# Sparse attention and a gated feed-forward layer on one core: the first 21 transfers wait for the landing of the third one ahead

## The chip, the cores and the metric

One core of a Trainium2 chip. The time is the device time of one execution in microseconds (us), the median of several runs. TensorE is called PE, VectorE DVE, ScalarE ACT, GpSimd POOL, and SyncE, which issues nearly all transfers of this kernel, SP.

## The reference, cut to what matters

```python
# q, k, v: 8 batches, 8 heads, 576 positions, head size 64, f32
scores = q @ k.T / sqrt(64)
# heads 0-3: only the last 32 positions; heads 4-7: only positions a multiple of 32 back
scores = where(mask, scores, -1e9)
attn   = softmax(scores)             # rowmax subtracted, divided by (rowsum + 1e-9)
x      = (attn @ v) laid out as (8*576, 512)
h      = x @ w_in                    # w_in 512 x 2048
out    = (h * sigmoid(h)) @ w_out    # w_out 2048 x 512
```

## The kernel before

The kernel first gathers keys, queries and values on the host into 6 groups per batch (three of the local kind, three of the strided kind). The device does the attention of batch 0 at the start, one group at a time, and that of the other batches between the matrix products of the feed-forward layer. The layer's weights are split into an upper and a lower part in a 32-bit format that PE multiplies fast, and each product is done as three (upper by upper, upper by lower, lower by upper).

Every piece of work is a named step with an engine. A planner (`Steps.arrange`, line 297) goes through them with assumed costs and due times and writes one order; `tile` then puts the instructions of each engine in that order and adds the semaphores. So each engine, SP included, works strictly in the order of the plan, and a step that waits holds back everything behind it on its engine. The planner also has a model of how PE's instructions are brought into it, block by block: `FETCHED, FIRST, AHEAD_BY = 256, 140, 309` and `FETCH = 10.0, 6.0` (lines 127 and 128). Block k is asked for when PE comes to its instruction 140 + 256 k, PE can go on for 309 instructions past that point without it, and the block is assumed to come 10.0 us after it was asked for in the first 40 us and 6.0 us later on. A matrix product counts as two instructions, one that loads weights and one that multiplies.

The opening, up to the first product of the layer (step `h0`, line 755), has these steps. `k`: a load of keys and queries, line 496 or 499. `S`: scores on PE, line 569. `M`: scaling, mask and row minimum on DVE, line 588. `E`: exponentials on ACT, line 597 or 609. `R`, `N`: row sums and scaling on DVE. `T`: transposes on PE, line 626. `P`: ACT copies them out of PSUM, line 632. `v`: a load of values, line 503. `O`: the products with the values on PE, line 688, in two of the groups behind four or five products with zeros (line 672). `B`: ACT places them in x, lines 706 and 723. `H`, `L`: the upper and lower part of x. `p`: a load of a 512 KB piece of the weights, line 474 (w_in) or 479 (w_out). `a` (ACT, lines 438 and 443), `j`, `b`, `d`: the rounding and splitting of that piece. `h0` needs `d0`, hence `a0` and `p0`; the product after the next needs `d3`, hence `p3`.

All loads go through one name, `load`, which is `nc.sync.dma_start`. SP issues them in this order (number, step, KB):

| | | | |
|---|---|---|---|
| 1 k5.5 334 | 2 k1.1 448 | 3 k2.2 448 | 4 k3.3 442 |
| 5 k 160 | 6 k0.0 320 | 7 p4 512 | 8 p2 512 |
| 9 p1 512 | 10 v5.5 192 | 11 v2.2 384 | 12 k4.4 442 |
| 13 v3.3 256 | 14 p5 512 | 15 k6.3 442 | 16 v0.0 384 |
| 17 v1.1 384 | 18 p0 512 | 19 v4.4 256 | 20 k6.0 448 |
| 21 p3 512 | 22 p7 512 | 23 p11 512 | 24 p6 512 |

The 21 together are 8,412 KB, 401 KB each on average. `tile` has eight semaphores for transfers and gives them out in turn; a transfer that takes one over waits at its issue for the landing of the one that had it, which is the eighth ahead of it. `p7` also waits for its buffer, that is for `d1`, and `p6` for `d0`. A tile called `w` in the rows is here a place of weights that a load of keys, queries or values borrows in the opening.

Of the kernel before, what the change touches and what calls it, by code (L numbers as in the profile page):

```python
# [55 lines left out]
OPS = 5  # L56
SMOOTH = 2
UNITS = 3


WAYS1 = (("A11", "B11"), ("S2", "T2"), ("S3", "T3"), ("A22", "T4"),
# [291 lines left out]
def sparse_attention_ffn(ctx: ExitStack, tc: tile.TileContext, kqt, vt, w_in, w_out, out, out_t):  # L353
    nc = tc.nc
# [98 lines left out]

    copy = {"DVE": nc.vector.tensor_copy, "ACT": nc.scalar.copy, "POOL": nc.gpsimd.tensor_copy}

    load = nc.sync.dma_start


    pieces = [(0, 0)]
# [367 lines left out]
    def do(*args, **kwargs):  # L827
        return steps.do(*args, **kwargs)
# [209 lines left out]
    def chunk_steps(fc):  # L1038
        due = begin + pace * fc

        def first():
            state["ph", fc] = hidden(fc, x, range(NP // 2))

        def second():
            hidden(fc, x, range(NP // 2, NP), state["ph", fc])

        def turn():
            state["th", fc] = tanh(state["ph", fc])

        def gated():  # L1050
            gate(state["ph", fc], state["th", fc])

        def gated_high():
            state["g", fc] = g_high(state["th", fc], engine=h.engine)

        def gated_low():
            g_low(state["th", fc], state["g", fc])

        ha = do(f"h{fc}", {"PE": 1.37}, first, reads=[("x", 0), ("x", 1)], after=[split_at[0, fc], *prior("h", fc)],
                takes=["ph"], due=due)  # L1060
        hb = do(f"i{fc}", {"PE": 1.37}, second, reads=[("x", 2), ("x", 3)], after=[ha], due=due)
        t = add(f"t{fc}", {"ACT": 0.5}, due - 5, [hb, *prior("t", fc)], turn, takes=["th"])
        g = add(f"g{fc}", {"DVE": 0.73}, due - 4, [t], gated, gives=[ha])
        steps.ends(ha, "ph", [g])
        h = add(f"w{fc}", {"DVE": 0.46, "ACT": 0.57}, due - 4, [g, *prior("w", fc)], gated_high, takes=["g"])
        d = add(f"l{fc}", {"DVE": 0.62}, due - 4, [h], gated_low)
        steps.ends(t, "th", [d])
        return hb, h, d

    made = [chunk_steps(fc) for fc in range(NFC)]  # L1070
# [244 lines left out]
    def add_unit(n):  # L1315
        if n >= len(units):
            return
        layer, name, half = units[n]
        tag, _, fcs = unit_names[n % UNITS]

        def go():
            at = const.tile([P, 4, 2, Q], F32R, name=tag)
            load(out=at.bitcast(F32), in_=ops_dram[layer][half][KEPT[layer].index(name)])
            unit_tiles[n] = at

        free = [("w", 0, fc) for fc in fcs] if n < UNITS else []
        do(f"u{n}", {"SP": 4.2}, go, reads=[("ops", layer, name, half)],
           writes=[("unit", n % UNITS), *free])

# [251 lines left out]
    def add_pair(p, bursts):  # L1581
# [16 lines left out]
        for first, ways in ((0, WAYS1[:4]), (4, WAYS1[4:])):  # L1598
            for half in range(2):
                z = {}  # L1600
                for i, _ in enumerate(ways, first):
# [3 lines left out]
                    for jp in (2 * half, 2 * half + 1):  # L1605
# [4 lines left out]
                        def go(i=i, jp=jp, z=z[jp], u=u, fresh=fresh):  # L1610
# [3 lines left out]
                            for jj in range(2):  # L1614
# [9 lines left out]
                        s = do(f"A{p}.{i}.{jp}", {"PE": 2.73}, go,  # L1624
                               reads=[("unit", u % UNITS), ("hi", (n0 + i) % OPS), ("lo", (n0 + i) % OPS)],
                               writes=[("z", z[jp])], takes=[zt_name[z[jp]]] if fresh else [])
# [4 lines left out]
                        if last:  # L1631
                            steps.ends(state["holder", z[jp]], zt_name[z[jp]], [end])
                    add_unit(u + UNITS)
                    after_op(p, n0 + i if half else -1)
# [4 lines left out]
        for i, _ in enumerate(WAYS2):  # L1639
# [6 lines left out]
            for jp in range(4):  # L1646
# [18 lines left out]
                final = (p, i) == (PAIRS - 1, 6)  # L1665
                reads = [("unit", u % UNITS), ("hi", slot), ("lo", slot)]
                if final:
# [87 lines left out]
    def after_op(p, n):  # L1755
        spent.add(n)
        while todo and todo[0] - OPS in spent:
            q, m = divmod(todo[0], 35)
            if m >= 7:
                i, jp = divmod(m - 7, 4)  # L1760
                if f"A{q}.{6 if i else 4}.{jp}" not in steps.by_name:
                    return
                g_op(q, i, jp)
            elif m != 3:
                x_ops(q)(m)
            todo.pop(0)
# [154 lines left out]
```

## Time and profile before

| | us |
|---|---|
| median of 3 runs | 813.5 |
| lowest and highest of the 3 | 810.86, 815.22 |
| span of the profiled execution | 811.7 |
| PE busy in it | 795.8 |
| DVE busy | 570.9 |
| ACT busy | 474.1 |

The profiled execution is one more execution, of which the page tells the span, from the first to the last instruction on an engine, and no device time beside it. A span leaves out what lies around the program, and the runs alone spread over 4.4 us. The busy times are unions over the whole span and say nothing of one stage; the opening, some 33 us, is read on its own below.

### The profile page before, as it was taken

Reading aid. Unit: us, or ns where it says so; the run is one execution under the profiler, and the core shown is the slowest. Engines: PE = TensorE matmul, PEld = TensorE weight load, DVE = VectorE, ACT = ScalarE, POOL = GpSimd, SP = SyncE. Lnnn points to the kernel's source line nnn. Section 1 sums busy time; section 2 is a strip of 40 time slices with the busy share of each in tenths; the row PEclk is TensorE's granted clock in tenths of the full one; section 3 lists DMA queues with packets and bytes.
Section 4 is the critical chain, followed back from the end, with each engine's and each line's share of the span. In section 5 each row is a group of like instructions: output and inputs, shape, how many; then the busy total and the mean of one; then the engine's idle time right before and its main releaser. Section 6 shows DMA issues by size and latency. Waiting matters only on the chain.

```text
span 811.7 us, 17628 instructions
## 1 busy us (share of the span) xinstructions
PE 795.8 (98%) x6909; PEld 655.1 (81%) x6909; DVE 570.9 (70%) x1371; ACT 474.1 (58%) x1160; POOL 60.2 (7%) x68
## 2 busy tenths in 40 slices
PE   5999999999999999999999999999999999999998
PEld 4788888888878888788888888888888888888886
DVE  6999976778988888733899866227867640389663
ACT  7988754636566557767678554555545344445441
POOL 2000000012100212000221100000000000000000
PEclk9999999999999999999999999999999999999999
DMA  9798888878776878798887877664575675554652
GB/s 328 272 325 249 248 229 258 273 198 237 223 238 192 239 256 262 223 244 282 280 267 261 259 262 264 211 220 179 191 228 186 238 235 180 203 208 176 215 223 111
DMA packets 113123, 190.21 MB, mean 234 GB/s; under 512 B 42896, under 2 KB 87696, under 8 KB 102288
## 3 DMA queue, kind: packets, MB, share of 16 engines
q1 hardware_dynamic: 113040, 189.08, 72.5%
q8 instruction: 54, 0.88, 0.4%
q14 instruction: 29, 0.24, 0.1%
HBM read 141.08 MB, written 38.80 MB: 222 GB/s over the span
## 4 chain that ended last, share of the span: by engine, by line
PE 87%; DVE 5%; ACT 3%; DMA 2%; issue 1%; POOL 1%; POOLq 0%; DVEq 0%; ACTq 0%
PE z L1658 28%; PE z L1618 27%; PE ph L755 13%; PE po L802 13%; PE pa L569 3%; ACT sm L597 1%; DMA sm<-pt 1%; PE z L688 1%; DVE stage L1179 1%; PE pa L688 1%; DVE g L782 1%; PE ph L688 1%; PE po L688 1%; DVE stage L1207 1%; DMA ops<-stage 1%
## 5 line engine op out<-in xcount | busy, mean ns | idle before, releaser
L1618 PE MATMUL z<-w,w 128*128 128x512 f32 x720 | 166.3, 390 | 0.0
L1618 PEld LDWEIGHTS z<-w,w 128*128 128x128 f32 x720 | 134.8, 188 | 28.1
L1658 PE MATMUL z<-w,w 128*128 128x512 f32 x576 | 134.1, 389 | 0.0
L1658 PEld LDWEIGHTS z<-w,w 128*128 128x128 f32 x576 | 108.0, 188 | 22.5
L755 PE MATMUL ph<-xhi,w 128*128 128x512 f32 x384 | 123.4, 391 | 0.0
L597 ACT ACTIVATE sm<-sm,sums 128x64 f32<-128x64 f32 x304 | 101.4, 339 | 8.5 <-DVE sums L588 7.6
L802 PE MATMUL po<-w,g 128*128 128x512 f32 x432 | 104.4, 392 | 0.2 <-DVE g L782 0.2
L802 PEld LDWEIGHTS po<-w,g 128*128 128x128 f32 x432 | 80.2, 188 | 17.7 <-DVE g L782 0.8
L1484 DVE TENSOR_TENSOR w<-w,w 128x1024 fp32r<-128x1024 f32 (+3 forms) x68 | 78.3, 1163 | 12.3 <-ACT w L1555 9.7
L755 PEld LDWEIGHTS ph<-xhi,w 128*128 128x128 f32 x384 | 72.1, 188 | 15.3
L755 PE MATMUL ph<-xlo,w 128*128 128x512 f32 x192 | 74.7, 389 | 0.0
L1513 DVE TENSOR_TENSOR w<-w,z 128x1024 f32<-128x1024 f32 x30 | 36.6, 1218 | 35.8 <-PE z L1618 35.6
L1555 ACT CAST w<-w 128x1024 fp32r<-128x1024 f32 (+1 forms) x40 | 39.2, 987 | 35.3 <-PE z L1658 33.8
L597 ACT ACTIVATION_READ_ACCUMULATOR sm<-sm,sums 128x1 f32 x304 | 58.2, 191 | 0.0
L1501 ACT ACTIVATE w<-w 128x1024 f32<-128x1024 f32 x30 | 31.8, 1062 | 39.5 <-DVE w L1513 39.2
L662 POOL COPY pt<-sm 128x896 uint16<-128x896 uint16 (+1 forms) x21 | 29.8, 1425 | 323.8 <-DMA sm<-pt 323.8
L1658 PE MATMUL z<-xhi,w 128*128 128x512 f32 x216 | 52.2, 390 | 0.0
L1658 PE MATMUL z<-xlo,w 128*128 128x512 f32 x216 | 52.2, 390 | 0.0
L1507 ACT COPY w<-z 128x1024 f32<-128x1024 f32 x30 | 30.4, 1014 | 35.9 <-PE z L1618 35.7
L765 ACT ACTIVATE th<-ph 128x512 f32<-128x512 f32 x48 | 28.4, 593 | 34.6 <-DVE g L782 19.5
L1658 PEld LDWEIGHTS z<-xhi,w 128*128 128x128 f32 x216 | 40.5, 188 | 8.4
L1658 PEld LDWEIGHTS z<-xlo,w 128*128 128x128 f32 x216 | 40.5, 188 | 8.4
(172 smaller groups left out, 1173.9 us busy)
## 6 DMA issues: line engine op xcount, KB each, us to landing
w<-ops SPq DMA_DIRECT2D x84, 1024.0 KB, 5.0
ops<-stage SPq DMA_DIRECT2D x48, 256.0 KB, 2.8
kd<-kqt SPq DMA_DIRECT2D x23, 448.0 KB, 5.5
ops<-w SPq DMA_DIRECT2D x80, 128.0 KB, 4.4
vd<-vt SPq DMA_DIRECT2D x24, 384.0 KB, 5.7
stage<-w_out SPq DMA_DIRECT2D x16, 512.0 KB, 5.8
stage<-w_in SPq DMA_DIRECT2D x16, 512.0 KB, 7.1
kd<-kqt SPq DMA_DIRECT2D x14, 442.0 KB, 5.6
```

The costliest lines, as they stand in the source:

```text
L597: nc.scalar.activation(out=self.s_sb[:, c, r], in_=self.s_sb[:, c, r], func=AF.Exp, bias=self.nmax[:, c, r : r + 1], scale=-1.0, accum_out ...
L662: copy[engine](out=self.halves(self.pt)[:, half], in_=came[:, half])
L688: nc.tensor.matmul(self.pso[b][to, at : at + wide], vds[v][half, tile_], self.pt[half, q0 : q0 + wide], start=True, stop=True,)
L755: nc.tensor.matmul(ph, weight(0, wi, fc)[:, cc * P : (cc + 1) * P], x[xi][:, cc], start=(cc, n) == (0, 0), stop=(cc, n) == (NP - 1, 2),)
L802: nc.tensor.matmul(po[tt], g[gi][:, cols], weight(1, wi, fc), start=fc == 0 and n == 0, stop=fc == NFC - 1 and n == 2,)
L1484: nc.vector.tensor_tensor(out=o, in0=x, in1=y, op=op1)
L1501: nc.scalar.activation(out=o, in_=x, func=AF.Silu)
L1507: nc.scalar.copy(out=o, in_=x)
L1513: nc.vector.tensor_add(o, x, y)
L1555: nc.scalar.copy(out=hi, in_=x)
L1618: nc.tensor.matmul(zt[z][:, jj], w[:, at, wi, cc * P : (cc + 1) * P], op[:, xi, cc], start=fresh and (cc, n) == (0, 0), stop=(cc, n) == (1 ...
L1658: nc.tensor.matmul(zt[zz][:, ds], w[:, at, wi, ds * P : (ds + 1) * P], op[:, gi, jj], start=fresh and (jp, jj, n) == (0, 0, 0), stop=(jp, ...
```

## The change

`load` becomes a function. It keeps a list of the transfers issued so far. A transfer that is number 4 to number 21 on this list gets a dependency, with a semaphore, on the transfer three ahead: SP waits before it issues number n until number n - 3 has landed. From number 22 on nothing is added. The order of the plan, the buffers and the work stay as they are.

```diff
+OPEN, EAGER = 3, 21
...
-    load = nc.sync.dma_start
+    moved = []
+
+    def load(**kwargs):
+        made = nc.sync.dma_start(**kwargs)
+        if OPEN <= len(moved) < EAGER:
+            tc.add_manual_dep(
+                made.ins, moved[-OPEN].ins.name,
+                mybir.DependencyInfo(mybir.DependencyClass.Sync, mybir.DependencyReason.DATA),
+                reason="few transfers under way",
+            )
+        moved.append(made)
+        return made
```

## Rows read from the trace of the kernel before

**Rows 1.** The page: busy time of each engine over the span.

```profile
PE 795.8 (98%) x6909; PEld 655.1 (81%) x6909; DVE 570.9 (70%) x1371; ACT 474.1 (58%) x1160; POOL 60.2 (7%) x68
```

**Rows 2.** Windows, opening and rest: busy us per engine, PE clock, DMA share, GB/s.

```profile
0.00:33.00 33.00, 22.48 (x574) 17.58 (x575) 23.62 (x119) 25.74 (x84) 4.92 (x25) 1.00 0.85 302
33.00:800.00 767.00, 765.41 (x6302) 631.31 (x6302) 545.86 (x1250) 448.39 (x1077) 55.33 (x43) 1.00 0.73 234
```

**Rows 3.** The chain that ended last, 18 to 33 us: start, us, what.

```profile
20.69 0.84 PE po L688 x29
21.53 1.21 issue
...
23.24 0.92 ACT xb L723 x2
...
32.78 0.43 PE ph L755
```

**Rows 4.** Timeline of SP in the opening: start, us, issue.

```profile
0.74 0.68 SPq L496 DMA_DIRECT2D w<-kqt  x1
...
2.10 0.41 SPq L496 DMA_DIRECT2D kd<-kqt  x1
2.56 0.55 SPq L496 DMA_DIRECT2D w<-kqt  x1
...
6.01 0.74 SPq L474 DMA_DIRECT2D stage<-w_in  x1
...
7.94 0.33 SPq L503 DMA_DIRECT2D vd<-vt  x1
...
18.12 0.38 SPq L474 DMA_DIRECT2D stage<-w_in  x1
```

**Rows 5.** DMA view by moment of issue: transfers 1, 2, 3, 9 and 21; KB, us to landing.

```profile
w<-kqt SPq DMA_DIRECT2D x1, 334.0 KB, 3.4
kd<-kqt SPq DMA_DIRECT2D x1, 448.0 KB, 4.1
kd<-kqt SPq DMA_DIRECT2D x1, 448.0 KB, 5.8
stage<-w_in SPq DMA_DIRECT2D x1, 512.0 KB, 8.9
```

**Rows 6.** Windows inside the opening, columns as in rows 2.

```profile
4.50:6.50 2.00, 1.51 (x72) 1.12 (x64) 0.12 (x1) 0.00 (x0) 1.62 (x8) 1.00 0.92 267
15.00:21.00 6.00, 5.62 (x133) 4.69 (x135) 5.61 (x15) 6.00 (x19) 0.00 (x0) 1.00 1.05 399
```

**Rows 7.** DMA queue of PE's instructions: page, then 20.3 to 20.4 us; packets, MB, share.

```profile
q8 instruction: 54, 0.88, 0.4%
...
q8 instruction: 1, 0.02, 58.8%
```

**Rows 8.** Timeline: step S3's weights on PE. Windows to 11.15 us, columns as in rows 2.

```profile
9.10 1.28 PEld L569 LDWEIGHTS po<-w 64*64 64x64 f32 x48 [0.33 <-DMA w<-kqt]
...
0.00:11.15 11.15, 4.90 (x200) 3.85 (x200) 3.88 (x49) 5.79 (x28) 4.92 (x25) 1.00 0.79 273
```

**Rows 9.** Timeline of ACT and PE: P5, a2, O1, a0, a3; idle before in brackets.

```profile
13.07 0.48 ACT L632 COPY th<-po 128x384 f32<-128x384 f32 x1 [0.34 <-PE po L626]
...
13.97 0.66 ACT L438 ACTIVATE stage<-stage 128x512 f32<-128x512 f32 x1
...
25.57 1.51 PE L688 MATMUL po<-th,vd 64*64 64x32 f32 x48 [0.68 <-ACT th L632]
...
26.85 0.69 ACT L438 ACTIVATE stage<-stage 128x512 f32<-128x512 f32 x1
...
30.53 0.69 ACT L438 ACTIVATE stage<-stage 128x512 f32<-128x512 f32 x1
```

**Rows 10.** DMA view at 142.4 and 74.6 us: loads issued behind another one.

```profile
kd<-kqt SPq DMA_DIRECT2D x1, 448.0 KB, 4.8
...
stage<-w_in SPq DMA_DIRECT2D x1, 512.0 KB, 3.7
```

## The prediction

> **What bounds the kernel now.** I read the page first. PE is busy for 795.8 of the 811.7 us of the span [rows 1], so little is to be won outside it. The windows then say where its idle time lies. From 33 to 800 us PE works 765.41 of 767 us. In the first 33 us it works 22.48, so 10.5 us of the kernel's idle time stand in the opening [rows 2]. The change touches transfers 1 to 21, the last of which is issued at 18.12 us [rows 4], all of it in this opening. After it PE has no hole into which a delay could sink. So whatever moves the first product of the layer, `h0`, which the chain reaches at 32.78 us [rows 3], moves the end by as much, and nothing else that the change does can count. The granted clock is 1.00, the 2.4 GHz level, in the opening and after it, with PE busy only 1.51 of 2 us from 4.5 to 6.5 us [rows 2, 6]; I put no clock term into the sum.
>
> In the chain of the opening, ACT and PE take turns. Transfers set the pace only at the very start: the scores of group 3 begin at 9.10 us, 0.33 us after the engine came free, when transfer 4 lands [rows 8]. Then ACT works nearly without a break. Late in the opening one step is neither work nor a wait for data: 1.21 us of "issue" on PE at 21.53, in the middle of step `O3`, of which 29 products were done and 3 left [rows 3]. ACT waits for these 3 to place them, and starts that at 23.24; the rest of the opening hangs on it.
>
> That hole looks like missing instructions. PE's queue of instructions moved 54 packets and 0.88 MB [rows 7] for 6,909 loads of weights and 6,909 products [rows 1], that is 256 instructions a packet. The second block that the opening needs moved at 20.3 us [rows 7]. By the planner's count it is asked for at instruction 396, the 198th product. By 11.15 us 200 products have begun [rows 8], so the request falls at about 11.1 and the packet moves some 9.2 us later. The data transfers of that time take 8.9 us from issue to landing [rows 5], with eight under way: transfer 11 is issued at 7.94, as transfer 3 (2.10 plus 5.8) lands [rows 4, 5].
>
> **The change, part by part.** Transfer 4, issued at 2.56, now waits for transfer 1, which lands at 0.74 + 3.4 = 4.1; so the change is not idle [rows 4, 5]. From there to number 21 three are under way instead of eight. The other waits are implied by this one. Behind a waiting transfer on SP stand only later transfers: 22, 23 and 24 are pushed back with number 21, no other engine issues loads here, and the 18 added waits cost no engine but SP, which does nothing else.
>
> The cost is the pace of landings. Before, number 9 lands at 6.01 + 8.9 = 14.9 and number 21 at 18.12 + 8.9 = 27.0 [rows 4, 5]: 12 transfers in 12.1 us, 1.0 us each, with the DMA engines full (399 GB/s) [rows 6]. With three under way a transfer is issued when the third ahead lands, so the pace is a third of the time from issue to landing, or 1.0 us if that is longer. The trace has no steady stretch of three such loads. Its nearest rows bound it. Below: transfer 1, with nothing ahead, takes 3.4 us [rows 5], for 401 KB some 3.6 (67 KB more at 399 GB/s), a pace of 1.2; the floor is the full engines' 1.0. Above: a load of 448 KB issued behind another takes 4.8 us in mid-kernel [rows 10], a pace of 1.6; another of 512 KB takes 3.7 there [rows 10], 1.25. Transfer 2, with one ahead in this very opening, takes 4.1 us [rows 5], a pace of 1.37. I take 1.28, between transfers 1 and 2, which are the opening's own, and keep 1.0 and 1.6 for the range.
>
> The start gains a little. Transfer 3 now lands without five others issued behind it; the engines moved only 267 GB/s while these crowded in [rows 6]. It can land no earlier than 448 KB at 399 GB/s (1.15 us) after transfer 2 (1.47 + 4.1 = 5.6, as its issue is not changed), at 6.7, and no later than now, at 7.9. I take 7.3 and let the others follow at 1.28 us each. Against the moments at which each is used now:
>
> - number 4: 8.6, used at 9.10 [rows 8]: 0.5 earlier, but the copy at 13.07 had waited only 0.34 us [rows 9], so at most that reaches ACT
> - number 8, p2: 13.7, used at 13.97: in time
> - number 17, v1.1: 25.2, used by `O1` at 25.57
> - number 18, p0: 26.5, used by `a0` at 26.85
> - number 21, p3: 30.3, used by `a3` at 30.53 [rows 9]
>
> All are in time, by 0.2 to 0.4 us, where the spare was several us (p3 landed at 27.0). The spare is the cover that this change spends: at a pace of (30.53 - 7.3) / 18 = 1.29 nothing is lost at p3, eighteen transfers after number 3, and each 0.1 more costs 1.8 us.
>
> The gain is the 1.21 us hole. A block of instructions that waits as the transfers do would come with them in about 4 us instead of 9.2, at 15 to 16 us, long before PE runs dry. Then `O3` ends 1.2 us sooner and ACT goes on sooner. But what is late next is the loads themselves: v1.1 allows `O1` only 0.4 us earlier than now, p0 allows `a0` 0.35, and p3 allows `a3` 0.2. So 0.2 us of 1.2 are kept.
>
> A rule of the Trainium skill bears on this, and nothing else here is built on it. The page DMA: Bandwidth & Descriptors, in Anatomy of one DMA, gives a transfer about 2.0 us and its bytes at 436 GB/s, for the GpSimd path; by that, as an estimate, 401 KB take 2.9 us, three under way keep the engines full, and the sum would be the full gain of the first rival. Transfer 1 took 3.4 us for 334 KB, so the trace is slower than the rule.
>
> **The sum.** The profiled execution has a span of 811.7 us, 1.8 under the median of the runs, a difference inside their own spread. 811.7 - 0.2 = 811.5 of span, and 813.5 - 0.2 = 813.3 of time. Measurement of this kernel can tell about 0.5% (4.07 us) from no change.
>
> **The rivals.**
>
> *Full pace.* The landings keep 1.0 to 1.15 us each. At 1.1, v1.1 lands at 7.3 + 14 x 1.1 = 22.7, p0 at 23.8, p3 at 27.1; none binds, the hole closes for 1.2 us, and up to 0.34 us more comes from the early scores. Time: 812.0 to 812.3. For it: full engines at 1.0; against it: no load in the opening landed in under 3.4 us. Chance 0.20.
>
> *The pace collapses, slower.* At 1.6 a transfer, p3 lands at 7.3 + 18 x 1.6 = 36.1, 5.6 us after `a3` starts now. ACT works in order, so everything behind `a3` waits, the last parts of x for the first products among it, and PE stands still. Time: 819.1. It leaves the 0.5% at 4.07 us, that is from a pace of (30.53 + 4.07 - 7.3) / 18 = 1.52. For it: the 4.8 us row of mid-kernel; against it: that stretch also carries stores, and the opening's own two rows stay under 4.1. Chance 0.15.
>
> *The hole stays.* The block of instructions does not wait behind data, so fewer transfers free nothing. The hole's 1.21 us remain and the landings are in time: 813.5. For it: the packet itself is one of 54 and tiny; against it: 9.2 us of delay beside transfers of 8.9. Chance 0.12. The Trainium skill has a rule of this kind on the same page, in Queues, rings and completion order: each DMA engine takes the queues in turn, packet by packet; by it a block would not stand behind eight transfers, and by my count of the request the trace does not agree (9.2 us).
>
> *The forecast*, landings a little late but inside the spare, or over it by less than 4 us: 0.53.
>
> **How the numbers follow.** Only the collapse leaves the half per cent; faster than 809.4 needs more than the whole hole and early gain, 1.5 us, and is left to scatter. Faster 0.04, same 0.81, slower 0.15. The range: at the low end the full pace, 812.0, less a scatter of about 1.5 (the three runs spread 4.4): 810.5. At the high end it takes in most of the slow paces: a pace of 1.5 costs 7.3 + 27 - 30.53 = 3.8, so 817.3, rounded to 817.5.
>
> **What would show it.** Right: transfers 4 to 21 take 3.5 to 4.5 us to land; transfer 4 is issued near 4.1; the "issue" step at 21.5 is gone; the instruction block moves near 16 us; `a3` starts between 29.5 and 31 and `h0` within 1 us of 32.78. Wrong: latencies near 5 us, ACT or PE waiting for w_in or v loads between 24 and 33 us, and `h0` after 36; or a change in the stretch from 33 to 800 us, which would mean that the shift of the opening has upset the plan behind it.

## The result, and the profile after

| us | before | after |
|---|---|---|
| median of 6 runs each | 813.56 | 818.17 |
| lowest and highest | 810.86, 815.22 | 816.27, 820.09 |
| span of the profiled execution | 811.7 | 817.6 |

The changed kernel is slower: ratio 1.006, 95% interval 1.0046 to 1.0073. Of 813.56 us that is 4.9 us (the two medians lie 4.6 apart), more than the half per cent that was called the bound, and the median lies just above the range on record. The span is some 1.8 us under the time of the same execution in every run (817.6 and 819.37 here), so the 1.8 us in the prediction's sum are no scatter. Of the cases forecast, *The pace collapses* describes it. The rest of this part shows that in the trace, in the order of the rows of before.

The page's busy time, beside [rows 1]: no engine has more work worth naming.

```profile
PE 796.4 (97%) x6909; PEld 654.1 (80%) x6909; DVE 572.2 (70%) x1371; ACT 475.7 (58%) x1160; POOL 60.0 (7%) x68
```

Windows of the changed kernel, columns as in [rows 2]. The opening is cut at 38 us here, since the layer begins later; the rest is a stretch of the same 767 us.

```profile
0.00:38.00 38.00, 22.31 (x577) 17.60 (x578) 23.73 (x119) 25.75 (x83) 4.92 (x25) 1.00 0.80 254
38.00:805.00 767.00, 765.35 (x6296) 629.60 (x6295) 546.72 (x1250) 449.94 (x1077) 55.11 (x43) 1.00 0.74 234
```

In 767 us from 38 on, PE works 765.35, against 765.41 before. So the loss stands in the opening: about the same work on every engine, spread over some 5 us more.

The chain that ended last, 10 to 45 us, beside [rows 3]: where ACT and PE took turns before, one transfer now waits for another.

```profile
10.72 5.28 DMA stage<-w_in
...
16.01 7.06 DMA w<-kqt
...
23.16 3.75 DMA kd<-kqt
...
26.92 4.49 DMA stage<-w_in
...
31.43 4.42 DMA stage<-w_in
...
35.87 0.71 ACT stage L439
...
43.30 1.89 PE ph L767 x7
```

These are transfers 9 (p1), 12 (k4.4), 15, 18 (p0) and 21 (p3): every third one, which is what the added wait ties together. From 10.72 to 35.85 us the chain is nothing but issue, landing, next issue.

The timeline of SP, beside [rows 4]: transfer 4, then 12, 13, 14, then 15.

```profile
3.98 2.58 SPq L460 DMA_DIRECT2D w<-kqt  x2
...
16.01 0.55 SPq L460 DMA_DIRECT2D w<-kqt  x1
16.60 0.60 SPq L460 DMA_DIRECT2D w<-vt  x1
17.98 0.38 SPq L460 DMA_DIRECT2D stage<-w_in  x1
23.16 0.55 SPq L460 DMA_DIRECT2D kd<-kqt  x1
```

The view of the transfers by moment of issue, beside [rows 5] (KB, us to landing): numbers 12 and 13, then 15.

```profile
w<-kqt SPq DMA_DIRECT2D x1, 442.0 KB, 7.1
w<-vt SPq DMA_DIRECT2D x1, 256.0 KB, 7.1
...
kd<-kqt SPq DMA_DIRECT2D x1, 442.0 KB, 3.8
```

Number 3 lands at 7.08 us and number 21 at 31.43 + 4.42 = 35.85: 18 transfers in 28.77 us, 1.60 us each, where the forecast had 1.28. The windows show the engines short of work, beside [rows 6]:

```profile
15.00:20.00 5.00, 4.08 (x79) 3.14 (x78) 3.87 (x11) 5.00 (x14) 0.00 (x0) 1.00 0.81 230
20.00:25.00 5.00, 1.79 (x64) 1.82 (x64) 2.40 (x16) 2.44 (x11) 0.00 (x0) 1.00 0.46 137
```

Timeline of PE and ACT, beside [rows 9]: S4, O3, O1, a0, a3, the first products with w_out, and the first product of the layer (its listing gives count, ns, first and last start).

```profile
23.20 1.14 PE L581 MATMUL pa<-w 64*64 64x64 f32 x32 [3.21 <-DMA w<-kqt]
24.08 1.10 PE L700 MATMUL po<-th,w 64*64 64x54 f32 x32
...
30.31 1.51 PE L700 MATMUL po<-th,vd 64*64 64x32 f32 x48 [2.47 <-DMA vd<-vt]
...
31.44 0.68 ACT L439 ACTIVATE stage<-stage 128x512 f32<-128x512 f32 x1 [2.43 <-DMA stage<-w_in]
...
35.87 0.71 ACT L439 ACTIVATE stage<-stage 128x512 f32<-128x512 f32 x1 [0.67 <-DMA stage<-w_in]
...
46.16 1.07 PE L814 MATMUL po<-w,g 128*128 128x512 f32 x4
...
L767 PE MATMUL ph<-xhi,w x24: 388/392/499, 37.1 to 45.9; 128*128 128x512 f32 x24
```

PE waits 3.21 us for k4.4 and 2.47 for v1.1, ACT 2.43 for p0. `a0` starts at 31.44 instead of 26.85, `a3` at 35.87 instead of 30.53, `h0` at 37.1 instead of 32.7: 4.4 of the 5.9 us by which the profiled span grew. Part of the rest arises just behind `h0`. The chain above leads over DVE's work on p3 and on x to the products at 43.30, and the first product with w_out begins at 46.16, 9.0 us after `h0`, where before it began 8.3 after it (41.03). That is 0.7 of the other 1.5 us; the last 0.8 arise later, and where is not shown.

`O3` shows no hole: its 32 products stand in one row, where 29, a hole of 1.21 and 3 stood before. But the block of instructions did not come sooner, as the queue's row of 20.3 to 20.5 us shows, beside [rows 7]; the packet starts at 20.41 us. `O3` begins at 24.08 instead of 20.47, after the block is there.

```profile
q8 instruction: 1, 0.02, 29.3%
```

### The profile page after: what moved, and what is told of

It is laid out like the page before. It is cut to its first block, busy times and chain, and to the rows that moved or that the text cites. A ratio compares the mean times of both kernels' runs of the same rounds, so it can differ in the third digit from the quotient of the medians.

```text
span 817.6 us, 17627 instructions
## 1 busy us (share of the span) xinstructions
PE 796.4 (97%) x6909; PEld 654.1 (80%) x6909; DVE 572.2 (70%) x1371; ACT 475.7 (58%) x1160; POOL 60.0 (7%) x68
## 4 chain that ended last, share of the span: by engine, by line
PE 89%; DMA 6%; DVE 3%; ACT 1%; issue 0%; SPq 0%; DVEq 0%; ACTq 0%
PE z L1670 28%; PE z L1630 27%; PE po L814 15%; PE ph L767 14%; PE pa L581 3%; DMA stage<-w_in 2%; DMA kd<-kqt 2%; PE ph L700 1%; DMA w<-ops 1%; PE z L700 1%; DMA w<-kqt 1%; PE pa L700 1%; DVE stage L1191 1%; DMA out<-osb 1%; DVE sm L600 0%; DVE xlo L759 0%
## 5 line engine op out<-in xcount | busy, mean ns | idle before, releaser
L1525 DVE TENSOR_TENSOR w<-w,z 128x1024 f32<-128x1024 f32 x30 | 36.5, 1218 | 37.2 <-PE z L1630 37.1
```

What stands on the lines that cost most here:

```text
L1525: nc.vector.tensor_add(o, x, y)
```

## The experiments

Two theories of the 1.60 us were set against each other. The *latency theory* (theory B where an expectation has letters): a load takes a time to land of which a large part does not depend on what else is under way, so with n under way the pace is that time over n. The *late-engine theory* (A): three under way would nearly do, but a transfer lands with the slowest of 16 engines, and one engine falls some 3 us behind around a block of PE's instructions; eight under way hide that and three do not. For the second spoke the stretch behind transfers 12 to 14 in the changed kernel, 23.35 to 24.5 us:

```profile
DMA packets 28, 0.03 MB, mean 26 GB/s; under 512 B 0, under 2 KB 28, under 8 KB 28
...
q1 hardware_dynamic: 28, 0.03, 7.3%
```

26 GB/s is about what one engine in 16 has of the 399 of [rows 6] (24.9), and 7.3% of the time of 16 engines is 1.2 engines at work. The theory reads this as one engine that works off its rest of transfer 14 while the two loads issued at 23.16 and 23.75 have hardly begun to move. Which engine moved a packet the trace does not show.

**1. The changed kernel again.** No edit.

> The changed kernel once more, for a second profile. Theory A (a transfer lands with the slowest of the 16 DMA engines, and one engine falls back by some 3 us near each load of PE's instructions): the gap in the flow between 18 and 24 us comes again, transfers 12 to 14 take about 7 us again, the span is within 1 us of 817.6. Theory B (each transfer pays a fixed time from issue to landing of some 4.3 us, and a third of that is the pace): transfers 12 to 14 take about 4.3 us like the others, transfer 21 lands near 7.1 + 18 x 1.42 = 32.7 instead of 35.9, and the span is near 815.

820.7 us, span 818.9, 1.3 above the first. The gap is there again, and number 21 lands at 35.83, as theory A expected and not B. So the lag at 12 to 14 belongs to the kernel and is no accident of one execution.

```profile
stage<-w_in SPq DMA_DIRECT2D x1, 512.0 KB, 7.1
...
w<-vt SPq DMA_DIRECT2D x1, 256.0 KB, 7.4
```

**2. Only transfers 4 to 9 wait.**

```diff
-OPEN, EAGER = 3, 21
+OPEN, EAGER = 3, 9
```

> Only transfers 4 to 9 wait. Theory A and theory B both: the loss of pace (about 0.35 us each, 2 us in all at number 9) stays inside the spare of the later loads, transfer 21 lands at 27 to 28 us, time within 2 us of the kernel before, 812 to 815. If the early waits are what costs, 816 or more. If the first loads landing sooner is a gain of its own, 812 to 813.

814.78 us (10 runs; before 812.9 on that chip), ratio 1.0022, interval 1.001 to 1.0034. p3 lands at 30.0, later than the 27 to 28 expected but in time. p2 lands at 15.1 (used at 13.97 before) and v5.5 at 17.4 (before, its products began at 15.75), both late. `h0` starts at 34.8. The chain shows that the hole has not gone; it has grown:

```profile
21.84 0.84 PE po L700 x29
22.68 1.76 issue
24.44 0.47 PE po L700 x3
```

**3. Only transfers 13 to 21 wait.**

```diff
-        if OPEN <= len(moved) < EAGER:
+        if 12 <= len(moved) < EAGER:
```

> Only transfers 13 to 21 wait. Transfer 12 lands near 17.5 as before. Theory A: the late engine near 20 us stops the flow for some 3.5 us, transfer 21 lands at 33 to 34, time 816 to 817. Theory B: 9 transfers at 1.42, transfer 21 lands near 30.3, which is inside the spare, time 813 to 814.

816.01 us (5 runs), ratio 1.0039, interval 1.002 to 1.0057. From number 12 (16.90) to number 21 (32.04) nine transfers take 15.1 us, 1.68 each, though none takes over 5.9 us. So the time is the one that theory A expected, but the cause it gave, a stop of 3.5 us, is not there; theory B had 1.42 and no loss, and missed. In this execution the block moves at 17.0 and the hole is gone, and what it gave is lost to p0, for which ACT waits:

```profile
28.21 0.65 ACT L439 ACTIVATE stage<-stage 128x512 f32<-128x512 f32 x1 [2.51 <-DMA stage<-w_in]
```

The losses of experiments 2 and 3, 0.22% and 0.39%, add up to the change's 0.6%, as far as intervals of such width can tell.

**4. The changed kernel with S1's products done twice**, which moves the blocks of instructions against the loads; the work is repeated.

```diff
-                    for r in range(2):
+                    for r in (0, 1) * (2 if (self.b, self.gis) == (0, (1,)) else 1):
```

> The changed kernel with the 24 score products of step S1 done twice into the same place (the result is the same, 48 products of PE's count more, 0.97 us on PE where it has spare). PE comes to the point at which it asks for its second block of instructions some 1.5 to 2 us earlier. Theory A with the instruction load as the cause: the packet of the block moves before 19.5 us instead of at 20.4, and the stretch in which one engine lags moves with it or changes its size by more than 1 us. Theory B, or a late engine with another cause: the lag stays at transfers 12 to 14 between 18 and 24 us wherever the packet goes. Span 816 to 819 either way.

827.75 us, one run, span 825.9, outside the 816 to 819 expected. The second block moves at 16.0 and transfers 12 to 14 land in about 4 us, in the same order of loads; transfer 5, under way at the first block (7.8 us), now takes 5 instead of 2.9. So a lag can go with a block, here with the first and not with the second. Yet p3 comes no sooner: ACT waits for it until 37.27, as the row below shows, which makes (37.25 - 6.92) / 18 = 1.69 us a transfer from number 3 on. The time says nothing of the loads: `h0` starts at 36.8, before the changed kernel's, and the rest is lost later, most of it in waits of PE, 4.6 us of them "issue".

```profile
37.27 0.68 ACT L439 ACTIVATE stage<-stage 128x512 f32<-128x512 f32 x1 [3.01 <-DMA stage<-w_in]
```

**5. The width of the window: one, two, four, five, six under way.** One and two were run once, four and five 10 times, six 12 times.

```diff
-OPEN, EAGER = 3, 21
+OPEN, EAGER = 1, 21     # and 2, 4, 5, 6
```

> Five under way instead of three, transfers 6 to 21. Two causes stand for the lost pace of 1.60 us a transfer. Latency theory: a load takes about 4.3 us to land however few are under way, so the pace is that over five, 0.9, and the full engines' 1.0 holds: number 21 lands by 28, nothing is late, 812.0 to 814.0. Late-engine theory: one of the 16 engines falls some 3 us behind at the blocks of PE's instructions, and five under way hide about 4 us: the same time, with latencies of 6 to 7 us at transfers 12 to 14 and a landing of k4.4 before 21. The two differ in that: by the first theory alone no transfer stands out there.

> Four under way, transfers 5 to 21. Latency theory: pace 4.3 / 4 = 1.08, number 21 lands near 7.5 + 17 x 1.08 = 25.9 to 27, no loss, 813 to 814. Late-engine theory: the lag of about 3 us is hidden for one part only; transfers 12 to 14 take 7 us again, number 21 lands at 28 to 30, k4.4 is 1 to 2 us late, 814 to 816.

> Two under way, transfers 3 to 21. Latency theory: a load with one ahead takes 3.5 to 4.2 us, so the pace is 1.75 to 2.1 and number 21 lands at 40 to 44 us; h0 near 41 to 45 and a time of 822 to 827. Late-engine theory alone, with loads of 1.2 us each and two lags of 3 us: number 21 at 33 to 36 and a time near 817 to 820.

> One transfer at a time, 2 to 21: each then shows its own time from issue to landing with nothing else on the engines. Latency theory: the greater part of it does not depend on what else is under way, 448 KB take about 3.3 us and 192 KB no less than 2.3, so the pace is about 3.2 and number 21 lands near 4 + 20 x 3.2 = 68 us; the time is near 850. If the latencies of 4.3 with three under way came from sharing the engines, a lone load of 448 KB takes 2.2 or less (its bytes at 399 GB/s are 1.15 us), the pace is near 2, number 21 lands near 44 and the time is near 827.

> Six under way, transfers 7 to 21. With five the pace was 1.12 us, the hole in O3 was gone, the layer's first product came 1.2 us sooner and the time was the same as before. Latency theory: 5.6 to 6 us over six is the engines' full pace of 1.0; nothing is late. Then 812.3 to 813.5, the low end if the block of instructions again comes by 18 us and what it gives is kept, the high end if it comes at 20 as before or if it is lost again at a later block. Late-engine theory: the same, no lag shows.

| under way | 3 lands | 21 lands | us a transfer | that times the number under way | `h0` | time, ratio |
|---|---|---|---|---|---|---|
| 1 | 10.52 | 70.14 | 3.31 | 3.3 | 68.4 | 854.84 |
| 2 | 7.38 | 43.90 | 2.03 | 4.1 | 44.5 | 827.13 |
| 3 (the change) | 7.08 | 35.85 | 1.60 | 4.8 | 37.1 | 818.17, 1.006 |
| 4 | 7.64 | 32.56 | 1.38 | 5.5 | 34.8 | 815.6, 1.0018 (1.0006 to 1.0029) |
| 5 | 7.19 | 27.32 | 1.12 | 5.6 | 31.6 | 813.62, 1.0004 (0.9995 to 1.0014) |
| 6 | 7.35 | 26.92 | 1.09 | 6.5 | 33.4 | 812.71, 1.0005 (0.9992 to 1.0018) |
| 8 (before) | 7.9 | 27.0 | 1.06 | 8.5 | 32.7 | 813.56 |

The fifth column is what a transfer takes from issue to landing on the mean, since with n under way the next is issued when the n-th ahead lands. From one to four it goes 3.3, 4.1, 4.8, 5.5: close to a straight line, 2.6 us and 0.74 more for each one under way, itself included. By it the pace is 2.6 / n + 0.74, which five and six beat a little (1.26 and 1.17 by the line), until the full engines hold it near 1.0. That is the latency theory, with a part added for each neighbour. The line is a fit to one execution each, and its point for three holds the lag at 12 to 14: those take 7.00 us from the landing of 11 to that of 14, the other fifteen 1.45 us each, that is some 4.3 us from issue to landing. (The medians of the kernel before beside these were 813.3 and 813.5; a ratio weighs all runs.) The loads of the kernel with one under way, 31 to 56 us, show what a load costs with nothing beside it (KB, us to landing), and the window below them what the engines then carry:

```profile
vd<-vt SPq DMA_DIRECT2D x3, 384.0 KB, 2.9
stage<-w_in SPq DMA_DIRECT2D x2, 512.0 KB, 4.2
w<-kqt SPq DMA_DIRECT2D x1, 442.0 KB, 3.3
...
w<-vt SPq DMA_DIRECT2D x1, 256.0 KB, 2.6
w<-vt SPq DMA_DIRECT2D x1, 192.0 KB, 2.4
```

```profile
31.00:56.00 25.00, 7.48 (x152) 6.00 (x155) 9.47 (x36) 8.80 (x23) 0.00 (x0) 1.00 0.41 124
```

192 KB take 2.4 us and 384 take 2.9: halving the bytes saves 0.5 us. (The two of 512 KB took 3.5 and 4.95.) At 399 GB/s the bytes of 192 KB are 0.5 us and those of 384 KB 1.0, so some 1.9 us of either are not bytes. The engines deliver 124 GB/s of 399.

With two, the chain from 5 to 44 us is transfers nearly alone, none far above the others (3.1 to 4.9 us); its last:

```profile
39.36 4.54 DMA stage<-w_in
```

The late-engine theory alone had expected number 21 at 33 to 36 us; it landed at 43.90, where the latency theory had 40 to 44. With one it had 68 us and a time near 850, measured 70.14 and 854.84.

With five the listing of ACT's waits from 6.5 to 45 us (us, times, longest) has one for a load, 0.4 us; PE has no "issue" in `O3` and begins the layer 1.1 us sooner:

```profile
ACT stage L439 <- DMA stage<-w_out: 0.4, 1, 0.4
```

```profile
L767 PE MATMUL ph<-xhi,w x32: 389/389/500, 31.6 to 45.1; 128*128 128x512 f32 x32
```

The time does not show that 1.1 us. With six the block of instructions comes at 20.06 us, the hole stands again in the chain, 1.27 us at 21.24, and the time is the same. With four the hole is there too, 0.86 us. Four was a miss of the latency theory: it expected no loss and 1.08, by a latency of 4.3 that does not grow with the number under way, and measured 1.38 and 0.18%.

**6. Only transfers 13 to 16 wait.**

```diff
-OPEN, EAGER = 3, 21
+OPEN, EAGER = 3, 16
-        if OPEN <= len(moved) < EAGER:
+        if 12 <= len(moved) < EAGER:
```

> Only transfers 13 to 16 wait for the third ahead; 4 to 12 and 17 to 21 are issued as before the change. With 13 to 21 waiting the block of instructions came at 17.0 instead of 20.3 us, the hole in O3 was gone, and yet p0 and p3 landed too late. If the block comes sooner because it does not stand behind eight transfers, it does so here too: it moves at 17 to 18 us, the hole of 1.21 us is gone, and p0 and p3, issued at 20 to 22, land by 29.5: h0 at 31.5 to 32.5, 812.0 to 813.3. If the earlier block was an accident of one execution, it moves at 20 or later, the hole stays, and the time is 813.3 to 814.5.

The block moves at 17.66 and the hole in `O3` is gone. What that gave is spent on loads, as in experiment 3: `O1` waits for v1.1 and `a0` for p0, and `h0` starts at 32.9.

```profile
25.37 1.51 PE L700 MATMUL po<-th,vd 64*64 64x32 f32 x48 [1.07 <-DMA vd<-vt]
...
26.58 0.67 ACT L439 ACTIVATE stage<-stage 128x512 f32<-128x512 f32 x1 [1.19 <-DMA stage<-w_in]
```

p3 lands at 29.70, in time; but 816.26 us (10 runs), ratio 1.0027, interval 1.0014 to 1.004. Neither expectation fits. The profiled execution took 814.1, less than all but one of the other nine runs, so its trace does not show where the usual run loses its 2 us. That is left open.

**7. The changed kernel with 16 products of S1 done twice.** That work is repeated.

```diff
-                    for r in range(2):
+                    for r in (0, 1) * (2 if (self.b, self.gis) == (0, (1,)) and t < 8 else 1):
```

> The changed kernel with 16 products of S1 done twice: that work is repeated, nothing else is altered. PE then comes 16 products sooner to the end of each block of its instructions; with 48 repeated the second block moved at 16.0 instead of 20.4. Late-engine theory: the second block moves near 19 us, and the long latencies (7 us against 4 to 5) go with it, to transfers 11 to 13 instead of 12 to 14. Rival, a fixed place in the order of loads (the sizes or buffers of 12 to 14): the three stay at 12 to 14 with 7 us, wherever the block is.

822.89 us, one run. The block moves at 15.7, not near 19. Transfers 12 to 14 take 5.4 to 5.7 us instead of 7, and the 7 us have not gone to 11 to 13; number 14, then 13:

```profile
stage<-w_in SPq DMA_DIRECT2D x1, 512.0 KB, 5.4
...
w<-vt SPq DMA_DIRECT2D x1, 256.0 KB, 5.6
```

The lag is smaller, but not gone. The flow falls here too, for 1 us, although the block moved at 15.7; below that row stand the changed kernel's 2 us:

```profile
22.50:23.50 1.00, 1.00 (x49) 1.00 (x46) 0.21 (x3) 0.37 (x3) 0.00 (x0) 1.00 0.29 48
...
22.50:24.50 2.00, 1.29 (x49) 1.32 (x52) 0.10 (x1) 0.00 (x0) 0.00 (x0) 1.00 0.11 38
```

And number 21 lands at 36.44, no sooner than with the full lag. Number 6 is issued at 6.92, when number 3 has landed: (36.44 - 6.92) / 18 = 1.64. So a fixed place in the order does not by itself make 7 us (experiment 4 has 4 us at the same place), and the 7 us at 12 to 14 do not set the pace: with three under way and a smaller lag there, or none, it is 1.69, 1.64 and, over the last nine, 1.68 (experiments 4, 7 and 3). What smaller lags add to it elsewhere is not shown. In the changed kernel itself, the fifteen transfers besides 12 to 14 kept 1.45, by which number 21 would have landed at 7.08 + 18 x 1.45 = 33.2, still 2.7 us after `a3` began before.

## Why the prediction was wrong

**The bound of the kernel: right in the main.** Most of the loss stands in the opening, and the 767 us behind it are as full after as before. That `h0` moves the end by as much, and that nothing else can count, holds only roughly: here `h0` moved by 4.4 us and the span by 5.9, with two under way by 11.8 and 13.6. With five `h0` came 1.1 us sooner and the end of the span 0.5.

**The start: right.** Transfer 4 issued at 3.98 (forecast 4.1), number 3 landed at 7.08 (7.3), number 4 at 8.21 (8.6).

**The pace of landings: the step that failed.** The rule of the step held: a third of the time from issue to landing, 4.8 / 3 = 1.60. The time put into it was wrong. It came from transfers 1 and 2, 3.6 us with nothing ahead and 4.1 with one ahead, and was divided by three as though the two neighbours cost nothing. Experiment 5 shows that each transfer under way adds some 0.74 us: a lone load takes 3.3 us, one of three 4.8. The very rows held the growth (3.4, 4.1, 5.8 for the first, second and third transfer [rows 5]), and the row of mid-kernel, 4.8 us behind another load [rows 10], gave 1.6, the measured value; it was kept only as the upper end. That it hit 1.6 exactly is in part luck, since that load had one other ahead and stores beside it, and the 1.60 holds the lag at 12 to 14, which no row of before shows. Without the three transfers of the lag, 1.45 a transfer would still have been over the 1.29 at which p3 is in time. The text set against it that the opening's own two rows stay under 4.1, and those are the rows with the fewest neighbours.

The Trainium skill's page DMA: Bandwidth & Descriptors, Anatomy of one DMA, which had been set beside this step, gives 2.0 us and the bytes at 436 GB/s; as an estimate that is 2.45 us for 192 KB and 3.2 for 512. The lone loads of experiment 5 agree with it roughly (2.4, and 3.5 for most of 512 KB), although the page's path is GpSimd's; with three under way the trace does not (2.9 to 7.1 us, 4.7 on the mean), so the full pace did not follow from it.

**What is late: right in kind, too short a list.** The signs of being wrong that the prediction gave are what came: latencies near 5 us, PE and ACT waiting for v1.1 and p0, `h0` after 36. v1.1, p0 and p3 were named and did come late, 4.6 to 5.3 us after the moments of use before. k4.4 and v5.5 were not on the list. By the forecast's own pace v5.5, number 10, would have landed at 7.3 + 7 x 1.28 = 16.3, after its use at 15.75; experiment 2 shows that the early waits alone cost 0.22%.

**The gain of the hole: wrong, and it did not matter.** The block was to come at 15 to 16 us because it waits as the transfers do. It moved at 20.41, and over all windows at 22.7, 20.4, 20.9, 18.1 and 20.1 us for two to six under way, 20.3 for eight: in no order of their number. In this the rival *The hole stays* was right. What sets its moment is not shown. That the hole is missing instructions, as the prediction read it, the runs bear out: in all thirteen traces PE has 12 waits of "issue" over 0.25 us, and each ends 2.2 to 2.8 us after a block's packet started (20.31 and 22.74 before, 22.00 and 24.44 in experiment 2, 20.06 and 22.52 with six, 202.77 and 205.19 in experiment 7). By that, `O3` of the changed kernel, which begins at 24.08, comes too late to meet the hole.

**The rival that came true.** *The pace collapses* put p3 at 36.1 and the time at 819.1; measured 35.85 and 818.17. It had a chance of 0.15, and the boundary it gave for leaving the half per cent, a pace of 1.52, lies between four and three under way (1.38 and 1.60), as the losses do (0.18% and 0.6%).

**Still open.** Why a lone load needs some 2 us beside its bytes, and a neighbour adds to that; what held back transfers 12 to 14, and whether the block of instructions did: experiment 4 speaks for that, 7 against it in part, since the flow fell near 23 us with the block at 15.7; where the usual run of experiment 6 loses its 2 us; and where the layer loses the 1.1 us that five under way win. No window beat the kernel before.

## What to carry to other kernels

With few transfers under way the pace is the time from issue to landing over their number, and that time is not a constant: measure it with as many neighbours as the change leaves, or take the row that has the most. Here 3.3 us for one became 4.8 for three and 5.5 for four, and only from five on did loads of 400 KB come near the engines' pace. When a change spends slack, list every user of every transfer concerned against the new landing times, not only the last ones.

## What the runs showed that was not expected

**A few products more, and waits far behind them.** With sixteen products more in the opening (experiment 7) PE stands 4.2 us in "issue" from 45 us on, where the list of the changed kernel has no such row. These waits, too, end 2.3 to 2.8 us after a block's packet starts. That the sixteen products shifted the places where blocks begin is the likely reason, but it is argued and not shown. The two largest rows of it, 3.9 us, in PE's waits there:

```profile
PE ph L700 <- issue: 3.0, 2, 1.6
PE z L700 <- issue: 0.9, 1, 0.9
```

**The clock of the opening.** The windows print 1.00 from the start, but the first entry of the clock in the trace of before is its rise to 1.00, the 2.4 GHz level, at 31.0 us, after PE had worked without a break from 25.57 on. In experiment 4 an entry says 0.50, the 1.2 GHz level, from 11.9 us to 35.8, and the 48 products of a values step take as long as in the opening of before, 1.51 us [rows 9]:

```profile
12.50:35.00 22.50, 15.35 (x290) 11.97 (x289) 16.83 (x59) 16.48 (x43) 0.00 (x0) 0.50 0.85 269
```

```profile
28.10 1.51 PE L700 MATMUL po<-th,vd 64*64 64x32 f32 x48 [1.90 <-DMA vd<-vt]
```

Behind the rise, in the kernel before, 48 such products and 32 larger ones together take less:

```profile
69.80 1.39 PE L688 MATMUL pa<-pt,vd 64*64 64x32 f32 x80
```

So the opening of before ran at the lower level too, and the prediction's sentence that its granted clock was 1.00 took a missing entry for a reading. The sums do not hang on it: their durations were measured.
